# Sparse attention with two gated layers: measured durations for small TensorE tasks in the table that a planner orders the instructions by

## The chip, the cores and the metric

The kernel runs on one core of a Trainium2 chip. The metric is the time of one execution on the device in microseconds (us); where several runs were made, the median stands first and the lowest and highest behind it. Five instruction queues matter here: TensorE (PE, matrix products), VectorE (DVE), ScalarE (ACT), GpSimd (POOL, masks at the start only) and SyncE (SP), which issues nearly all DMA transfers.

## The reference

Four batches of 576 positions with 8 heads of 64 go through a sparse attention: heads 0 to 3 look at the last 32 positions, heads 4 to 7 at positions with the same remainder modulo 32. The 2304 x 512 result goes through a layer with a Mish-like gate (512 to 2048 to 512), and then through a layer that takes the maximum of three products (512 to 768, back to 512). The weights are 64-bit numbers, which the kernel reads as two 32-bit words; every operand of the large products is split into a high and a low part (three products for one).

```python
scores = scale * np.matmul(q, k.transpose(0, 1, 3, 2))
mask_local = (rel >= 0) & (rel < stride)
mask_strided = (rel >= 0) & (pos[None, :] % stride == pos[:, None] % stride)
attn = np.exp(scores - max);  attn = attn / sum;  x = np.matmul(attn, v)
h = x @ w_in;  x = (h * np.tanh(softplus(h))) @ w_out
h = np.maximum(np.maximum(x @ w1, x @ w2), x @ w3);  out = h @ w_out
```

## The kernel before

The kernel never lets a scheduler order its instructions. `build_plan` describes the whole computation as some thousands of tasks: each has an engine, a duration (`cost`, in ns), the buffers that it reads and writes, a rank, and a function that emits its instructions. `Plan.run` then plays the tasks through on paper, engine by engine, always taking the ready task of lowest rank, forwards and backwards in turn; the forward order that ends first on paper is emitted as it stands. So a duration in this table changes no instruction. It changes where in each engine's queue an instruction stands.

**The attention** is cut into 48 units: 4 batches, 4 pairs of heads, 3 units each, of 3 or 4 tiles. A unit keeps one PSUM bank (`a0`, `a1`, `a2`, `acc1`, `acc2` in turn) and goes through: scores on PE (L413, two products a tile, one for each head, side by side in a quarter of the array each: the tiled mode), mask and row maximum on DVE (L426, L432), exponentials on ACT (L438), normalisation on DVE (L445 to L451), a transpose on PE (L458), its copy on ACT (L463), the product with v on PE (L471, tiled mode again), and the split of the result on ACT and DVE (L489, L493). The trace shows each tiled product as two records. q and k are loaded and turned beforehand: for batch 0 through PE (L355, tiles `early`), for the others by a DVE transpose (L329, tiles `raw`).

**The first product of the gated layer** for the first four slices of w_in (L516 in 288 columns, banks `h0` and `acc3`, 384 instructions) only needs finished attention rows and converted weights, and the planner weaves it in between the small tasks. The last 72 of these come behind the attention. Then follow L543 and L516 (the gated layer) and L590 and L615 (the second layer) in long unbroken rows.

**Fills.** Where the plan sees PE waiting, it puts in products that compute nothing (L839, 128x256 into `acc0`, which nobody reads), as many as fit in the wait by its own clock; they are there to keep the engine active. No fill is put in once the first L543 has been planned.

**What the planner charges on PE**: the cost of the task, and `SWITCH` where a task that is not tiled follows a tiled one; until this change a transpose counted as small and was free of it. The way back into the tiled mode is charged nothing. For a wait between engines it uses the table `WAIT`.

Of the kernel before, what the change touches and what calls it, by code (L numbers as in the profile page):

```python
# [19 lines left out]
P = 128  # L20
# [14 lines left out]
RES = 3  # L35
ATT_BANKS = ("a0", "a1", "a2", "acc1", "acc2")
RAW_BANKS = ("h0", "acc3")
RING = dict(h=3, g=3, ev=4, wt=4, s=5, st=8, pt=3, raw=2, qT=2, v=2)
# [5 lines left out]
    pe=dict(pe=0, act=200, dve=210, pool=200, sp=200), act=dict(pe=260, act=140, dve=150, pool=200, sp=150),  # L44
# [3 lines left out]
for waits in WAIT.values():  # L48
    waits["qa"] = waits["sp"]
WAIT["qa"] = dict(WAIT["sp"])  # L50
SWITCH = 60
DMA_ISSUE, DMA_START, DMA_END = 475, 1125, 850
HAM, HAM_COLS = 10240 / 3, 3060
SMALL_MM = ("scores", "tp", "av", "qkt")
# [13 lines left out]
class Plan:  # L68
# [30 lines left out]
    def run(self, rank, backward):  # L99
        succ, pred = (self.pred, self.succ) if backward else (self.succ, self.pred)  # L100
        n = len(self.name)
        left = [len(p) for p in pred]
        ready, done = [0.0] * n, [0.0] * n
        free = dict.fromkeys(self.ENGINES, 0.0) if backward else dict(START)
        later = {e: [] for e in self.ENGINES}
        now_ready = {e: [] for e in self.ENGINES}
        for i in range(n):
            if not left[i]:
                heappush(later[self.eng[i]], (0.0, i))
        order, wire, busy, last, fill, count = [], 0.0, {}, None, True, 0  # L110
        table = "mish" if backward else "exp"
        while count < n:
            now, e = min(
                (free[e] if now_ready[e] else max(free[e], later[e][0][0]), j)
                for j, e in enumerate(self.ENGINES) if now_ready[e] or later[e]
            )
            e = self.ENGINES[e]
            while later[e] and later[e][0][0] <= now:
                i = heappop(later[e])[1]
                heappush(now_ready[e], (rank[i], i))  # L120
            if e == "pe" and last is not None:
                def worth(entry):
                    name = self.name[entry[1]]
                    same = name == last if last in SMALL_MM else name not in SMALL_MM
                    return entry[0] - STAY * same, entry[1]

                r, i = min(now_ready[e], key=worth)
                now_ready[e].remove((r, i))
                heapify(now_ready[e])
            elif e == "act":  # L130
                def late(entry):
                    t = TABLE.get(self.name[entry[1]], table)
                    return entry[0] + TABLE_STAY * (t != table), entry[1]

                r, i = min(now_ready[e], key=late)
                now_ready[e].remove((r, i))
                heapify(now_ready[e])
            else:
                i = heappop(now_ready[e])[1]
            cost = self.cost[i]  # L140
            if e == "act":
                t = TABLE.get(self.name[i], table)
                cost += TABLE_LOAD * (t != table)
                table = t
            if e in ("sp", "qa"):
                free[e] = now + DMA_ISSUE
                wire = max(wire, now + (0 if backward else DMA_START)) + cost
                done[i] = wire + (DMA_START if backward else 0) + DMA_END
            else:
                if e == "pe":  # L150
                    t, w = free[e], int(free[e] // HAM)
                    fill = fill and not backward and self.name[i] != "x2_mm"
                    while fill and t + (c := FILL / (2.4 if busy.get(w - 1, 0) >= HAM_COLS else 1.2)) + FILL_GAP <= now:
                        busy[w] = busy.get(w, 0) + FILL
                        order.append(-1)
                        t += c
                        w = int(t // HAM)
                    if last in TILED_MM and self.name[i] not in SMALL_MM:
                        cost += SWITCH
                    last = self.name[i]  # L160
                    if not backward:
                        w = int(now // HAM)
                        busy[w] = busy.get(w, 0) + self.cols[i]
                        cost *= 1 if busy.get(w - 1, 0) >= HAM_COLS else 2
                done[i] = free[e] = now + cost
            order.append(i)
            count += 1
            for j in succ[i]:
                wait = WAIT[self.eng[j]][e] if backward else WAIT[e][self.eng[j]]
                ready[j] = max(ready[j], done[i] + wait)  # L170
                left[j] -= 1
                if not left[j]:
                    heappush(later[self.eng[j]], (ready[j], j))
        return order, done, max(done)
# [15 lines left out]
def build_plan(k, B, H, S, D, DM, FF, FF2, wide):  # L190
# [120 lines left out]
    def attention():  # L311
        n = 0
        for i, (b, hp) in enumerate(pairs):
            local = hp < 2
            r = i % 2
            rv = i if i < RING["v"] + 2 else i % RING["v"]
            rk0 = unit_rank(n)
            lr = rk0 - 8 if b else -200 + i
            if not b:
                early_qk(i, b, hp, local, r, rk0, lr)  # L320
            for nm in ("q", "k") if b else ():
                for g in range(4):
                    add("qk_load", "sp", S * PACKET[128], (lambda g=g, nm=nm, b=b, hp=hp, r=r: k.load_qk(nm, g, b, hp, k.raw(nm, r))),
                        writes=[("raw", nm, r, g)], rank=lr)

                def tr(nm=nm, r=r, local=local):
                    t = k.qkT(nm, r)
                    tv = t.rearrange("p (j r) -> p j r", r=STRIDE) if local else t.rearrange("p (r j) -> p j r", j=NJ)
                    nc.vector.transpose(out=tv, in_=k.raw(nm, r))  # L329

                add("tr", "dve", 669, tr, reads=[("raw", nm, r, g) for g in range(4)], writes=[("qT", nm, r)], rank=rk0 - 0.5)
            vparts = k.v_parts(hp)
            for j in range(vparts):
                v_cost = PACKET[256] * (LK * (2 if j == 0 else NL - 1) if local else NJ * (NS - (j % RES == RES - 1)))
                add("v_load", "sp", v_cost, (lambda j=j, b=b, hp=hp, rv=rv: k.load_v(j, b, hp, k.v(rv))),
                    writes=[("v", rv, j_) for j_ in range(j, 2 * RES, vparts)], rank=lr + 0.5)
            for u, tiles in enumerate(unit_tiles[local]):
                unit(n, i, u, tiles, b, hp, local, r, rv)
                n += 1
            if i == H // 2 - 1:  # L340
                add("hrpool", "dve", 0, k.open_hrpool, writes=[("earlypool",)], rank=-1)
# [35 lines left out]
    def unit(n, i, u, tiles, b, hp, local, r, rv):  # L377
# [31 lines left out]
        for j, tl in enumerate(tiles):  # L409
            def scores(j=j, tl=tl):  # L410
                kw = LK if local else width(tl)
                for h in range(2):
                    nc.tensor.matmul(  # L413
                        ps()[LQ * h:LQ * h + width(tl), j * K:j * K + kw],
                        lhsT=cols("q", h, tl), rhs=cols("k", h, tl), start=True, stop=True,
                    )
            add("scores", "pe", 212 if local else 142, scores, reads=[("qT", "q", r), ("qT", "k", r)], writes=[bk], rank=rk, cols=4 * (K if local else width(tl)))

        def mask():
            if not local:  # L420
# [35 lines left out]
        for j in range(nt):  # L456
            def tp(j=j):
                nc.tensor.transpose(ps()[:K, j * P:j * P + rows], sv()[:, j, :], k.ident[:rows, :rows])  # L458
            add("tp", "pe", 108 if local else 100, tp, reads=[sk[j]], writes=[bk], rank=rk)
        w_ = (nt - 1) * P + rows  # L460

        def evac():
# [3 lines left out]
        for j, tl in enumerate(tiles):  # L466
            def av(j=j, tl=tl):
                w = width(tl)
                kw = LK if local else w
                for h in range(2):  # L470
                    nc.tensor.matmul(  # L471
                        ps()[D * h:D * (h + 1), j * M:j * M + w],
                        lhsT=k.v(rv)[:kw, h, tl, :], rhs=k.buf(pb)[:kw, j * P + LQ * h:j * P + LQ * h + w],
                        start=True, stop=True,
                    )
            add("av", "pe", 160, av, reads=[pk] + [("earlypool",)] * (rv >= RING["v"]) + [("v", rv, j_) for j_ in range(2 * RES)], writes=[bk], rank=rk, cols=8 * width(tl) * K / P)

        def io(part):
            xv = k.x[:, part, hp, b * S:(b + 1) * S]
# [411 lines left out]
```

## Time and profile before

| | |
|---|---|
| median of 3 runs | 801.79 us (799.7 to 802.49) |
| the profiled execution, own time | 803.02 us |
| its span, first to last instruction | 801.2 us |
| PE busy | 793.7 us (99%) |
| DVE busy, ACT busy | 361.0 us (45%), 321.1 us (40%) |
| granted TensorE clock, mean | 1.000 (the level of 2.4 GHz) |

The span has three stages. Up to about 143 us it is the attention with the woven-in products; from there to about 500 us the gated layer; from there to the end the second layer. A busy PE says little by itself, since pipelined products overlap in the records and fills count too: the starts of its instructions, and what it waited for, are the better guide.

### The profile page before, as it was taken

To read this page: it belongs to the slowest core of one execution; us is meant where nothing else is said; L and a number is where in the kernel's file an instruction comes from. 1 tells how busy PE (TensorE), PEld (TensorE's weight loads), DVE (VectorE), ACT (ScalarE), POOL (GpSimd) and SP (SyncE) were. 2 spreads that over 40 slices of the span, in tenths; PEclk is the share of its full clock that TensorE was granted. 3 is DMA by queue.
4 is the path that set the end of the run, shared out by engine and by line. 5 is a ranking of instruction groups with operands and counts; after the bars stand their busy time and mean duration, and the time that the engine had idled before them with its cause. 6 is when DMAs were issued, how large, how long until landed. Compare 5 with 4: busy or idle time off the path is not lost.

```text
span 801.2 us, 12605 instructions
## 1 busy us (share of the span) xinstructions
PE 793.7 (99%) x5017; PEld 670.4 (84%) x5017; DVE 361.0 (45%) x769; ACT 321.1 (40%) x839; POOL 4.4 (1%) x22
## 2 busy tenths in 40 slices
PE   9999999999999999999999999999999999999998
PEld 7878888988888888888888889888888888888897
DVE  6998886895941311311221169981222221122222
ACT  5988878996731322321322257631110111110111
POOL 2000000000000000000000000000000000000000
PEclk9999999999999999999999999999999999999999
DMA  9787750944900100100010069300100010010010
GB/s 212 156 158 125 134 105 22 351 149 163 334 2 1 53 0 1 54 0 1 1 53 0 1 224 325 109 1 0 53 1 0 13 41 1 0 53 1 0 53 27
DMA packets 119690, 59.66 MB, mean 74 GB/s; under 512 B 91984, under 2 KB 110416, under 8 KB 119632
## 3 DMA queue, kind: packets, MB, share of 16 engines
q1 hardware_dynamic: 118448, 58.57, 26.2%
q8 instruction: 39, 0.64, 0.3%
q10 hardware_dynamic: 1184, 0.30, 0.2%
q14 instruction: 19, 0.16, 0.1%
HBM read 49.41 MB, written 9.44 MB: 73 GB/s over the span
## 4 chain that ended last, share of the span: by engine, by line
PE 88%; DMA 4%; SPq 3%; DVE 3%; ACT 1%; issue 1%; DVEq 0%; ACTq 0%
PE bank_acc L543 23%; PE bank_a L590 21%; PE bank_a L516 12%; PE bank_acc L615 9%; PE bank_h L516 7%; PE bank_h L590 7%; PE bank_acc L516 3%; DMA wslot<-in_moe_w_dram 1%; DMA v<-in_v_dram 1%; PE bank_a L413 1%; PE bank_a L471 1%; SPq L809 1%; PE bank_a L458 1%; PE bank_acc L413 1%; PE bank_acc L471 1%; DMA wslot<-in_moe_w_out_dram 1%
## 5 line engine op out<-in xcount | busy, mean ns | idle before, releaser
L543 PE MATMUL bank_acc<-g,wslot 128*128 128x512 f32 (+1 forms) x960 | 205.1, 369 | 1.5 <-DVE g L538 0.7
L543 PEld LDWEIGHTS bank_acc<-g,wslot 128*128 128x128 f32 x960 | 168.3, 188 | 33.6 <-DVE g L538 2.0
L590 PE MATMUL bank_a<-x,wslot 128*128 128x512 f32 (+1 forms) x816 | 173.2, 367 | 0.0
L590 PEld LDWEIGHTS bank_a<-x,wslot 128*128 128x128 f32 x816 | 142.4, 189 | 25.5
L538 DVE TENSOR_TENSOR g<-h,g 128x512 fp32r<-128x512 f32 (+1 forms) x80 | 50.9, 636 | 192.1 <-ACT g L537 192.0
L516 PE MATMUL bank_a<-x,wslot 128*128 128x512 f32 (+1 forms) x540 | 116.2, 368 | 0.0
L516 PEld LDWEIGHTS bank_a<-x,wslot 128*128 128x128 f32 x540 | 94.6, 189 | 16.8
L599 DVE TENSOR_TENSOR h<-bank_a,h 128x512 f32<-128x512 f32 (+1 forms) x46 | 29.1, 633 | 137.3 <-PE bank_a L590 137.3
L615 PE MATMUL bank_acc<-wslot,g 128*128 128x512 f32 x324 | 78.3, 389 | 0.0
L516 PE MATMUL bank_h<-x,wslot 128*128 128x288 f32 (+2 forms) x372 | 74.2, 338 | 0.0
L615 PEld LDWEIGHTS bank_acc<-wslot,g 128*128 128x128 f32 x324 | 60.4, 188 | 12.3
L535 ACT ACTIVATE h<-bank_a 128x512 f32<-128x512 f32 (+1 forms) x45 | 25.0, 554 | 108.8 <-PE bank_a L516 108.8
L516 PEld LDWEIGHTS bank_h<-x,wslot 128*128 128x128 f32 x372 | 58.5, 188 | 7.1
L601 ACT ACTIVATE g<-h 128x512 fp32r<-128x512 f32 (+1 forms) x30 | 17.6, 588 | 114.9 <-DVE h L599 114.9
L590 PE MATMUL bank_h<-x,wslot 128*128 128x512 f32 (+1 forms) x264 | 58.3, 370 | 0.0
L438 ACT ACTIVATE s<-s,st 118x54 f32<-118x54 f32 (+1 forms) x160 | 55.2, 348 | 7.0 <-DVE st L432 6.7
L590 PEld LDWEIGHTS bank_h<-x,wslot 128*128 128x128 f32 x264 | 46.7, 188 | 8.6
L537 ACT CAST g<-h 128x512 fp32r<-128x512 f32 (+1 forms) x80 | 46.1, 577 | 4.4 <-PE bank_acc L543 2.6
L253 ACT ACTIVATE wt<-wslot 128x512 f32<-128x512 f32 x56 | 37.9, 678 | 21.6 <-DVE wslot L281 9.6
L277 ACT CAST wslot<-wt 128x512 fp32r<-128x512 f32 x56 | 34.3, 620 | 14.7 <-DVE wt L267 14.3
L596 ACT COPY h<-bank_a 128x512 f32<-128x512 f32 (+1 forms) x22 | 12.0, 547 | 69.0 <-PE bank_a L590 69.0
L281 DVE TENSOR_TENSOR wslot<-wt,wslot 128x512 fp32r<-128x512 f32 x56 | 38.2, 684 | 2.6 <-ACT wslot L277 2.5
(71 smaller groups left out, 680.2 us busy)
## 6 DMA issues: line engine op xcount, KB each, us to landing
wslot<-in_moe_w_out_dram SPq DMA_DIRECT2D x22, 512.0 KB
wslot<-in_moe_w_dram SPq DMA_DIRECT2D x18, 512.0 KB
wslot<-in_moe_w_in_dram SPq DMA_DIRECT2D x16, 512.0 KB
out_dram<-wt SPq DMA_DIRECT2D x18, 256.0 KB
x2p<-ev SPq DMA_DIRECT2D x16, 256.0 KB
ev<-x2p SPq DMA_DIRECT2D x16, 256.0 KB
rawq<-in_q_dram SPq DMA_DIRECT2D x48, 72.0 KB
rawk<-in_k_dram SPq DMA_DIRECT2D x48, 72.0 KB
```

What stands on the lines that cost most here:

```text
L253: nc.scalar.mul(k.wt(r2).bitcast(F32), k.words(slot)[1].bitcast(F32), 2.0 ** -111)
L277: nc.scalar.copy(out=k.open_slot(slot)[:, 0, :], in_=k.wt(r2).bitcast(F32))
L281: nc.vector.tensor_tensor(out=s[:, 1, :], in0=k.wt(r2).bitcast(F32), in1=s[:, 0, :], op=ALU.subtract)
L438: nc.scalar.activation(sv()[:, j, :], sv()[:, j, :], AF.Exp, bias=mx()[:, j:j + 1], accum_out=dn()[:, j:j + 1],)
L516: nc.tensor.matmul(k.bank(hb)[:, :n], lhsT=wap(("in", f), a, c), rhs=k.x[:, q, c, t0:t0 + n], start=(c == 0 and m == 0), stop=(c == KC - 1 ...
L535: add(name, "act", act(n, psum=not stored), lambda: nc.scalar.activation(Hh(), src(), AF.Mish, scale=W_SCALE), reads=sread, writes=[HK], r ...
L537: add("gh", "act", act(n), lambda: nc.scalar.copy(out=g()[:, 0, :n], in_=Hh()), reads=[HK], writes=[G0], rank=s)
L538: add("gl", "dve", dve(n), lambda: nc.vector.tensor_tensor(out=g()[:, 1, :n], in0=Hh(), in1=g()[:, 0, :n], op=ALU.subtract), reads=[HK, G0 ...
L543: nc.tensor.matmul(k.bank(f"acc{c}")[:, :n], lhsT=wap(("out", f), a, c), rhs=g()[:, q, :n], start=(first and m == 0), stop=(last and m == 2),)
L590: nc.tensor.matmul(k.bank(hb)[:, :n], lhsT=wap((w_, f), a, c), rhs=k.x[:, q, c, t0:t0 + n], start=(c == 0 and m == 0), stop=(c == KC - 1 a ...
L599: add("m2", "dve", dve(n), (lambda hb=hb: nc.vector.tensor_tensor(out=m_(), in0=k.bank(hb)[:, :n], in1=m_(), op=ALU.max)), reads=[("bank", ...
L615: nc.tensor.matmul(k.bank(ab)[:], lhsT=k.g(rg)[:, a, c * P:(c + 1) * P], rhs=t[:, q, :], start=(f == 0 and m == 0), stop=(f == F2C - 1 and ...
```

## The change

Four kinds of tasks get other durations, and two lines of the mode change are altered. Scores fall from 212 or 142 ns a tile to 96 or 56, products with v from 160 to 64; transposes on PE rise from 108 or 100 to 124 or 106, the DVE transpose from 669 to 760 or 1200. `SWITCH` rises from 60 to 90 and is now charged ahead of a transpose too. No instruction of the computation is added or removed.

```diff
-SWITCH = 60
+SWITCH = 90
-                    if last in TILED_MM and self.name[i] not in SMALL_MM:
+                    if last in TILED_MM and self.name[i] not in TILED_MM:
                         cost += SWITCH
-                add("tr", "dve", 669, tr, reads=[("raw", nm, r, g) for g in range(4)], writes=[("qT", nm, r)], rank=rk0 - 0.5)
+                add("tr", "dve", 760 if local else 1200, tr, reads=[("raw", nm, r, g) for g in range(4)], writes=[("qT", nm, r)], rank=rk0 - 0.5)
-            add("scores", "pe", 212 if local else 142, scores, ...
+            add("scores", "pe", 96 if local else 56, scores, ...
-            add("tp", "pe", 108 if local else 100, tp, ...
+            add("tp", "pe", 124 if local else 106, tp, ...
-            add("av", "pe", 160, av, ...
+            add("av", "pe", 64, av, ...
```

What the planner makes of it: up to the last 72 products L516 behind the attention the order is another one on every engine; from there on all queues are the same, word for word. Fills (L839) rise from 61 to 168; 107 more, all of them in this first part.

PE, batch 0, around the transposes of the fourth pair's q (`earlyq_96`), before:

```order
L839 MATMUL bank_acc_105<-x 128x256 x7
L471 MATMUL bank_a_101<-pt_124,v_134 64x64 x6
L458 MATMUL bank_a_102<-ident,s_110 54x118 x4
L839 MATMUL bank_acc_105<-x 128x256 x7
L355 MATMUL bank_h_104<-ident,earlyq_96 128x96 x3
L355 MATMUL bank_acc_108<-ident,earlyk_97 128x96 x3
L458 MATMUL bank_a_103<-ident,s_111 54x118 x4
L839 MATMUL bank_acc_105<-x 128x256 x3
```

The same place, after:

```order
L839 MATMUL bank_acc_105<-x 128x256 x7
L471 MATMUL bank_a_101<-pt_124,v_134 64x64 x6
L839 MATMUL bank_acc_105<-x 128x256 x15
L355 MATMUL bank_h_104<-ident,earlyq_96 128x96 x3
L839 MATMUL bank_acc_105<-x 128x256 x13
L458 MATMUL bank_a_102<-ident,s_110 54x118 x4
L355 MATMUL bank_h_104<-ident,earlyq_96 128x96 x3
L839 MATMUL bank_acc_105<-x 128x256 x3
```

Between the same products with v and the same end of the turning there are 10 fills before (7 and 3) and 31 after.

PE, some 20 rows on, at the first scores of batch 1 (`bank_a_103`), before:

```order
L471 MATMUL bank_acc_106<-pt_124,v_135 64x54 x4
L471 MATMUL bank_acc_106<-pt_124,v_135 64x36 x2
L516 MATMUL bank_h_104<-x,wslot 128x288 x3
L413 MATMUL bank_a_103<-qTk_131,qTq_129 64x96 x6
L516 MATMUL bank_h_104<-x,wslot 128x288 x3
L516 MATMUL bank_acc_108<-x,wslot 128x288 x6
```

The same place, after:

```order
L471 MATMUL bank_acc_106<-pt_124,v_135 64x54 x4
L471 MATMUL bank_acc_106<-pt_124,v_135 64x36 x2
L839 MATMUL bank_acc_105<-x 128x256 x19
L413 MATMUL bank_a_103<-qTk_131,qTq_129 64x96 x6
L839 MATMUL bank_acc_105<-x 128x256 x8
L458 MATMUL bank_acc_107<-ident,s_113 54x118 x4
```

Where products of the gated layer stood, 27 fills stand now; some of those products moved ahead, the others behind.

SP, the loads ahead of the fourth pair's q (`wslot` are slices of w_in, 512 KB each; `early` q and k, `v` values), before:

```order
L790 DMA wslot_233<-in_moe_w_in_dram 128x4x256
L820 DMA v1_134<-in_v_dram 96x2x64
L826 DMA v1_134<-in_v_dram 96x8x64 x2
L790 DMA wslot_255<-in_moe_w_in_dram 128x4x256
L834 DMA v2_135<-in_v_dram 18x11x64 x2
L834 DMA v2_135<-in_v_dram 18x10x64
L809 DMA earlyq3_96<-in_q_dram 96x6x64 x2
```

The same stretch, after:

```order
L790 DMA wslot_249<-in_moe_w_in_dram 128x4x256
L826 DMA v1_134<-in_v_dram 96x8x64 x2
L790 DMA wslot_278<-in_moe_w_in_dram 128x4x256
L790 DMA wslot_282<-in_moe_w_in_dram 128x4x256
L834 DMA v2_135<-in_v_dram 18x11x64 x2
L790 DMA wslot_311<-in_moe_w_in_dram 128x4x256
L834 DMA v2_135<-in_v_dram 18x10x64
L809 DMA earlyq3_96<-in_q_dram 96x6x64 x2
```

Four slices of w_in now stand ahead of that load, where there were two.

## Rows read from the trace of the kernel before

**Rows 1.** The page: busy time by engine; granted clock in 40 slices.

```profile
PE 793.7 (99%) x5017; PEld 670.4 (84%) x5017; DVE 361.0 (45%) x769; ACT 321.1 (40%) x839; POOL 4.4 (1%) x22
...
PEclk9999999999999999999999999999999999999999
```

**Rows 2.** Stretches: length, busy PE, PEld, DVE, ACT, POOL, clock, DMA, GB/s.

```profile
0.00:12.70 12.70, 10.96 (x73) 9.65 (x74) 5.58 (x13) 3.66 (x10) 4.39 (x22) 1.00 1.00 194
12.70:60.00 47.30, 46.95 (x653) 38.51 (x651) 45.22 (x139) 41.80 (x172) 0.00 (x0) 1.00 0.84 170
60.00:143.50 83.50, 83.32 (x1142) 71.04 (x1139) 65.09 (x196) 67.61 (x283) 0.00 (x0) 1.00 0.53 101
143.50:153.10 9.60, 9.60 (x74) 9.60 (x74) 8.01 (x15) 9.43 (x21) 0.00 (x0) 1.00 1.05 381
...
465.00:501.00 36.00, 34.86 (x276) 33.52 (x276) 31.13 (x62) 24.37 (x51) 0.00 (x0) 1.00 0.93 308
...
760.00:801.20 41.20, 37.43 (x267) 35.00 (x265) 9.73 (x21) 6.42 (x15) 0.00 (x0) 1.00 0.11 39
```

**Rows 3.** All waits of PE for other engines: us in total, times, longest.

```profile
PE bank_acc L839 <- DVE x L855: 1.2, 1, 1.2
PE bank_acc L543 <- DVE g L538: 0.7, 2, 0.5
PE bank_h L355 <- DMA earlyq<-in_q_dram: 0.6, 1, 0.6
PE bank_acc L543 <- ACT g L537: 0.5, 2, 0.3
```

**Rows 4.** Timeline of PE behind the attention: start, duration, instructions.

```profile
142.49 1.12 PE L839 MATMUL bank_acc<-x 128*128 128x256 f32 x8
143.45 1.75 PE L516 MATMUL bank_h<-x,wslot 128*128 128x288 f32 x12
...
153.01 1.31 PE L543 MATMUL bank_acc<-g,wslot 128*128 128x512 f32 x5
```

**Rows 5.** Timeline of PE from 60 us.

```profile
60.01 0.66 PE L516 MATMUL bank_acc<-x,wslot 128*128 128x288 f32 x3
60.60 0.57 PE L471 MATMUL bank_a<-pt,v 96*64 96x64 f32 x12
61.10 1.07 PE L516 MATMUL bank_h<-x,wslot 128*128 128x288 f32 x6
62.10 0.61 PE L413 MATMUL bank_a<-qTk,qTq 64*54 64x54 f32 x16
```

**Rows 6.** Timeline of PE from 12 us.

```profile
12.74 1.19 PE L839 MATMUL bank_acc<-x 128*128 128x256 f32 x8
13.78 0.41 PE L355 MATMUL bank_acc<-ident,earlyk 96*128 96x96 f32 x3
...
14.66 0.49 PE L458 MATMUL bank_a<-ident,s 128*96 128x128 f32 x3
15.07 0.88 PE L413 MATMUL bank_acc<-qTk,qTq 64*64 64x96 f32 x16
```

**Rows 7.** The chain of waits in order of time: start, length, what.

```profile
12.31 1.71 SPq L790
...
26.46 0.50 SPq L790
...
59.36 3.40 DMA v<-in_v_dram
...
80.19 0.33 PE bank_a L458 x3
...
134.09 0.94 PE bank_acc L471 x28
```

**Rows 8.** PE by line and form: busy, mean ns, idle before.

```profile
L839 PE MATMUL bank_acc<-x 128*128 128x256 f32 x61 | 12.0, 337 | 1.2 <-DVE x L855 1.2
```

**Rows 9.** DVE by line and form.

```profile
L329 DVE STREAM_TRANSPOSE qTk<-rawk 128x576 f32<-128x576 f32 x12 | 12.1, 1007 | 0.6 <-DMA v<-in_v_dram 0.6
```

More of the change, by code (lines that the diff above doesn't have):

```diff
@@ L416, in scores @@
                     )
-            add("scores", "pe", 212 if local else 142, scores, reads=[("qT", "q", r), ("qT", "k", r)], writes=[bk], rank=rk, cols=4 * (K if local else width(tl)))
+            add("scores", "pe", 96 if local else 56, scores, reads=[("qT", "q", r), ("qT", "k", r)], writes=[bk], rank=rk, cols=4 * (K if local else width(tl)))
         def mask():
@@ L458, in tp @@
                 nc.tensor.transpose(ps()[:K, j * P:j * P + rows], sv()[:, j, :], k.ident[:rows, :rows])
-            add("tp", "pe", 108 if local else 100, tp, reads=[sk[j]], writes=[bk], rank=rk)
+            add("tp", "pe", 124 if local else 106, tp, reads=[sk[j]], writes=[bk], rank=rk)
         w_ = (nt - 1) * P + rows
@@ L475, in av @@
                     )
-            add("av", "pe", 160, av, reads=[pk] + [("earlypool",)] * (rv >= RING["v"]) + [("v", rv, j_) for j_ in range(2 * RES)], writes=[bk], rank=rk, cols=8 * width(tl) * K / P)
+            add("av", "pe", 64, av, reads=[pk] + [("earlypool",)] * (rv >= RING["v"]) + [("v", rv, j_) for j_ in range(2 * RES)], writes=[bk], rank=rk, cols=8 * width(tl) * K / P)
         def io(part):
```

## The prediction

> **What bounds the kernel now.** I read the page first, then the stretches, the waits of PE, and its timeline at a few places. The page gives PE 99% busy at the full granted clock in all 40 slices [rows 1], against 45% and 40% on DVE and ACT. Busy time of PE proves little, so the waits come next: in the whole execution PE waited 3.0 us for other engines (1.2 + 0.7 + 0.6 + 0.5), and 1.2 of these are the very start [rows 3]. In the stretches PE idles 0.35 us between 12.7 and 60 us and 0.18 us up to 143.5; later it loses some 1.1 us at 465 to 501 us and 3.8 us at the very end [rows 2]. The starts agree. In the timeline each row begins where the steps of the one before end: the 72 products L516 behind the attention take 153.01 - 143.45 = 9.56 us, 0.133 each [rows 4], and three or six of them between tiled products take 0.59 and 1.00 us, which is 3 x 0.133 and 6 x 0.133 plus 0.2 for the change of mode [rows 5]. So in the attention stage PE is not merely busy but out of slack: the end of that stage (143.45 us, where the last 72 products L516 begin) is the sum of what stands in its queue, plus the start.
>
> DVE and ACT are close behind in one part: 45.2 and 41.8 us of 47.3 between 12.7 and 60 us, and 65 and 68 of 83.5 behind it [rows 2]. And up to 59.36 us the chain of work runs through SP and transfers of v, not through PE [rows 7]. Both are near limits, but neither makes PE wait today.
>
> **What the change does to PE's queue.** No product is added or taken away; only the order of the first part changes, and from the 72 products on all queues are the same. So the rest, 801.2 - 143.45 = 657.7 us of the span, is carried over as it is, and the question is how long the first part gets. Its PE work is the same 312 products L516, the same scores, transposes and products with v; what differs is fills and changes of mode.
>
> Fills: 168 where there were 61. Eight of them take 143.45 - 142.49 = 0.96 us from start to start [rows 4], 0.12 each. The mean of one record is 337 ns and the group's busy time 12.0 us for 61 [rows 8]; these are no prices, since neighbours overlap in the records and the first fills wait. 107 x 0.12 = **+12.8 us**. The low bound is the pace of L516 for fewer columns, 0.133 x 256 / 288 = 0.118 us, so 12.6 us; the high bound are the eight near the start, 13.78 - 12.74 = 1.04 us [rows 6], 0.13 each, so 13.9 us.
>
> Changes of mode: the queue leaves the tiled mode and comes back 77 times before and 71 times after. The price of such a trip depends on what is in it. Through products L516: coming back costs 0.59 - 3 x 0.133 = 0.19 us; leaving shows as six pairs L471 in 0.50 us [rows 5], where 14 pairs in one piece take 0.94 [rows 7], so eight pairs more cost 0.44, a pair 0.055, and leaving 0.50 - 6 x 0.055 = 0.17. Together 0.36. Through transposes alone: three of them take 15.07 - 14.66 = 0.41 us ahead of scores [rows 6] and 0.33 ahead of a product [rows 7], so coming back is 0.08 to 0.1, with the leaving 0.27. Trips that end from a product or a fill rise from 41 to 54, those that end from a transpose fall from 36 to 17: 13 x 0.36 - 19 x 0.27 = **-0.4 us**. The bounds are -2.2 us (six trips fewer at 0.36 each, if all cost alike) and 13 x 0.36 - 19 x 0.17 = +1.4 us (if the way back from a transpose is free).
>
> In sum PE's queue gets **12.4 us longer**. A rule would put this lower: the Trainium skill, TensorEngine Tiling (Array Packing), Key Properties, says that a change of the tiling mode drains the engine, which by itself counts every trip alike; with six trips fewer at 0.36 us the sum would be 12.8 - 2.2 = 10.6 us. The rows agree that a change costs time, yet a trip through transposes is cheaper than one through products.
>
> **Why the planner does it.** Between 12.7 and 143.45 us PE really spends 130.75 us, of which 312 x 0.133 = 41.5 go to L516 and 44 x 0.12 = 5.3 to fills, so 84 us to the small tasks with their mode changes. The old table charged 27.8 us for scores (72 tiles and 88), 25.6 for products with v (160), 16.6 for transposes, 2.9 for turning q and k and 2.6 for 43 switches, 75 in all. The new one charges 11.8, 10.2, 18.3, 2.9, and 71 x 0.09 = 6.4, 50 in all. The durations are true for a product in a row of its kind, but the way back into the tiled mode has no price, and it is what the old numbers were padded with. The plan now sees a PE with some 25 us more room than before, finds waits, and fills them. On the chip PE is later than the plan thinks, so the things that the fills wait for are there by then.
>
> **Other terms.** The dearer DVE transpose is near the truth (12.1 us for 12, 1007 ns each over both kinds [rows 9], against 669) and costs nothing by itself. Two slices of w_in more stand ahead of the fourth pair's q on SP. One is 512 KB: at 381 GB/s (143.5 to 153.1 us) [rows 2] 1.4 us, at the 194 GB/s of the start 2.7 us; the issue itself takes 0.50 to 1.71 us [rows 7]. So that q lands 2.8 to 5.4 us later. What hides it: 70 fills instead of 31 stand ahead of its first use, 39 x 0.12 = 4.7 us, and some small tasks that used to stand behind it are ahead of it now; PE did not wait there before. So 0 us; if the cover were gone, up to 5.4 us. DVE and ACT have the same work in a stage that is 12.4 us longer, so they lose slack nowhere on the mean.
>
> Against the profiled execution: 803.02 + 12.4 = 815.4 us. That execution lies 1.2 us over the median; against the median of the runs it is 801.79 + 12.4 = **814.2 us**.
>
> **The rivals.**
> A, fills in time and new waits on top. The loads and the conversions of w_in moved ahead in the stretch where DVE is 96% busy [rows 2] and the chain runs through loads [rows 7]. If PE comes to q, or to the rows that DVE normalises, before they are ready, it waits up to 5.4 us more: 814.2 + 5.4 = 819.6 us. Against it speaks that PE itself is later at every step.
> B, the fills lie in the shade. If PE in truth waits up to 59.36 us for what the chain shows there, fills only take the place of waits. 81 of the 107 lie ahead of the same products with v that start at 60.60 us; with these for nothing 26 x 0.12 = 3.1 us are left: 804.9 us. Against it: recorded starts follow each other at constant steps there, and the list of waits has 0.6 us for a load in all [rows 3].
> C, the new order is better, and **faster**. Fills would have to cost next to nothing, slipping into the draining at a change of mode as tiled pairs run side by side; then six trips fewer (-2.2 us) and the waits of PE behind the start (-1.8 us) [rows 3] would show: 797.8 us. It decides at 2.2 / 107 = 0.02 us a fill; the timeline has 0.12 [rows 4].
> D, nothing moves: the planner's table is not what bounds, and the order differs in ways that cancel. It needs the same shade as B and the gains of C: 801.8 us.
> Nor can more fills win a higher clock: it is 1.00 in all stretches with 61 of them [rows 2].
>
> **How the numbers follow.** The forecast (fills paid in full, no new wait) 0.78; A 0.12; B 0.04; D 0.03; C 0.03. The forecast's own bounds: 12.6 - 2.2 = 10.4 us and 13.9 + 1.4 = 15.3 us, so 812.2 to 817.1 us, and 811.5 to 818 with what a median of few runs scatters (the three lie 2.8 us apart). With the larger part of A the range is 811.5 to 819. A measurement of this kernel tells some 0.3% (2.4 us) from no change. Faster by more 0.03 (C), within 0.03 (D), slower 0.94.
>
> **What would show it.** In the profile after, the last 72 products L516 should begin at about 156 us instead of 143.45, L543 9.6 us behind them, and the stretches behind should have the old lengths. The L839 group should have 168 instructions; its rows in the timeline should keep 0.12 us a fill; PE's waits should stay at about 3 us. DVE and ACT should have the same busy time and more waits for PE. The prediction is wrong if the first part grows by much less than the fills (B) or if waits for early q, for L451 or for L463 appear on PE (A).

## The result, and the profile after

| | before | after |
|---|---|---|
| median | 801.75 us (799.7 to 802.67, six executions) | 811.19 us (808.47 to 812.39, six executions) |
| the profiled execution, own time | 803.02 us | 808.47 us |
| its span | 801.2 us | 806.7 us |
| last 72 products L516 begin | 143.45 us | 149.97 us |

The changed kernel is slower: ratio 1.0112, interval 1.0098 to 1.0126, which is 9.4 us. The forecast was 12.4 us more (814.2 us, range 811.5 to 819.0): right in sign and in the main cause, 3.0 us too much, and the time lies 0.3 us below the range. The two profiled executions are 5.5 us apart only: that of before (803.02 us) lies above all six in the table, and that of after is the shortest of its six; the section on the experiments shows a good part of why.

The page of after: busy time by engine, granted clock in 40 slices, and the chain that ended last by engine; the first two rows of before are [rows 1].

```profile
PE 799.8 (99%) x5124; PEld 680.6 (84%) x5124; DVE 358.8 (44%) x769; ACT 322.1 (40%) x839; POOL 4.4 (1%) x22
...
PEclk9999999999999999999999999999999999999999
...
PE 95%; DMA 2%; DVE 1%; ACT 1%; SPq 0%; issue 0%; ACTq 0%
```

107 more instructions on PE, the same numbers of instructions on DVE and ACT and nearly their busy time: nothing else was added. The chain, which still ran through loads for part of the early stage before [rows 7], is PE for 95% now. On the page of before that row reads:

```profile
PE 88%; DMA 4%; SPq 3%; DVE 3%; ACT 1%; issue 1%; DVEq 0%; ACTq 0%
```

All waits of PE in after (us in total, times, longest), for [rows 3]:

```profile
PE bank_acc L839 <- DVE x L855: 1.2, 1, 1.2
PE bank_h L355 <- DMA earlyq<-in_q_dram: 0.6, 1, 0.6
PE bank_acc L543 <- DVE g L538: 0.5, 2, 0.4
PE bank_acc L355 <- DVE qTk L370: 0.3, 1, 0.3
PE bank_acc L355 <- DMA earlyk<-in_k_dram: 0.2, 1, 0.2
PE bank_acc L543 <- ACT g L537: 0.2, 1, 0.2
```

3.0 us in sum, as before. The load of q that the prediction worried about is in the list with the same 0.6 us.

Stretches of after (length, then busy PE, PEld, DVE, ACT, POOL with their instructions, granted clock, DMA share, GB/s), for [rows 2]:

```profile
12.70:60.00 47.30, 47.30 (x653) 41.81 (x650) 40.57 (x126) 38.21 (x158) 0.00 (x0) 1.00 0.82 166
60.00:150.00 90.00, 90.00 (x1225) 78.33 (x1224) 65.95 (x204) 71.08 (x290) 0.00 (x0) 1.00 0.51 96
150.00:159.60 9.60, 9.60 (x75) 9.60 (x74) 8.18 (x15) 9.42 (x21) 0.00 (x0) 1.00 1.05 383
```

From 12.7 us on PE has no idle time at all in the attention (0.35 and 0.18 us before). DVE fell from 45.22 to 40.57 us of 47.3: with more fills on PE the small tasks go by more slowly, so DVE has less to do per us.

Timeline of PE in after behind the attention (start, duration, instructions), for [rows 4]:

```profile
148.55 1.58 PE L839 MATMUL bank_acc<-x 128*128 128x256 f32 x12
149.97 1.74 PE L516 MATMUL bank_h<-x,wslot 128*128 128x288 f32 x12
...
159.54 0.85 PE L543 MATMUL bank_acc<-g,wslot 128*128 128x512 f32 x3
```

Twelve fills from 148.55 to 149.97, 0.118 each; the 72 products in 9.57 us (9.56 before); and behind their start 806.7 - 149.97 = 656.7 us of the span (657.7 before). So the difference arises ahead of the 72 (6.5 us), as forecast, but they were expected at about 156 us. The 1.0 us less behind them is scatter: a second execution of before, further down, has 656.2 us there with the same queues.

### The profile page after: what moved, and what is told of

The parts are those of the page before. It is cut to its first block, busy times and chain, and to the rows that moved or that the text cites. A ratio compares the mean times of both kernels' runs of the same rounds, so it can differ in the third digit from the quotient of the medians.

```text
span 806.7 us, 12825 instructions
## 1 busy us (share of the span) xinstructions
PE 799.8 (99%) x5124; PEld 680.6 (84%) x5124; DVE 358.8 (44%) x769; ACT 322.1 (40%) x839; POOL 4.4 (1%) x22
## 4 chain that ended last, share of the span: by engine, by line
PE 95%; DMA 2%; DVE 1%; ACT 1%; SPq 0%; issue 0%; ACTq 0%
PE bank_acc L543 23%; PE bank_a L590 21%; PE bank_a L516 13%; PE bank_acc L615 9%; PE bank_h L516 8%; PE bank_h L590 7%; PE bank_acc L516 4%; PE bank_acc L839 3%; PE bank_a L413 2%; PE bank_a L471 2%; PE bank_a L458 2%; PE bank_acc L413 1%; PE bank_acc L471 1%; DMA wslot<-in_moe_w_in_dram 1%; PE bank_acc L458 1%; DMA wslot<-in_moe_w_dram 1%
## 5 line engine op out<-in xcount | busy, mean ns | idle before, releaser
L516 PE MATMUL bank_a<-x,wslot 128*128 128x512 f32 (+1 forms) x540 | 116.2, 368 | 0.0
L516 PEld LDWEIGHTS bank_a<-x,wslot 128*128 128x128 f32 x540 | 94.6, 189 | 16.8
L516 PE MATMUL bank_h<-x,wslot 128*128 128x288 f32 (+2 forms) x372 | 74.5, 338 | 0.0
L516 PEld LDWEIGHTS bank_h<-x,wslot 128*128 128x128 f32 x372 | 58.6, 188 | 6.9
L253 ACT ACTIVATE wt<-wslot 128x512 f32<-128x512 f32 x56 | 37.9, 678 | 19.4 <-DVE wslot L281 9.4
```

Source lines behind the costliest of these rows:

```text
L253: nc.scalar.mul(k.wt(r2).bitcast(F32), k.words(slot)[1].bitcast(F32), 2.0 ** -111)
L516: nc.tensor.matmul(k.bank(hb)[:, :n], lhsT=wap(("in", f), a, c), rhs=k.x[:, q, c, t0:t0 + n], start=(c == 0 and m == 0), stop=(c == KC - 1 ...
```

## The experiments

Theory 1, the prediction's: fills and changes of mode are paid, and nothing else. Theory 2: the fills keep the granted clock up, so taking them out loses what it gains. Theory 3: the new order makes PE wait, and its fills stand in waits that would otherwise show.

**One part of the change alone, the durations of scores and products with v.** 166 fills.

```diff
-            add("scores", "pe", 212 if local else 142, scores, ...
+            add("scores", "pe", 96 if local else 56, scores, ...
-            add("av", "pe", 160, av, ...
+            add("av", "pe", 64, av, ...
```

> One part alone: scores and products with v get their new durations, everything else as before. The order has 166 fills (after: 168) and 79 trips out of the tiled mode (after: 71). Theory 1, the fills that a cheaper PE brings are the change's cost: 105 x 0.119 = 12.5 us of fills, 2 trips more at 0.25, less 1 to 4 us of small waits that vanish: 809 to 814 us. Rival, the cost comes from the mode rule and the transposes: 802 us.

Measured: 812.5 us, ratio 1.0141 (1.0124 to 1.0159), clock 1.000. These two lines alone cost 11.3 us over the 801.15 us of before in that session, more than the whole change.

**The rest of the change alone** (transposes dearer on PE and DVE, `SWITCH` 90, also charged ahead of a transpose). 62 fills, one more than before.

```diff
-SWITCH = 60
+SWITCH = 90
-                    if last in TILED_MM and self.name[i] not in SMALL_MM:
+                    if last in TILED_MM and self.name[i] not in TILED_MM:
-                add("tr", "dve", 669, tr, ...
+                add("tr", "dve", 760 if local else 1200, tr, ...
-            add("tp", "pe", 108 if local else 100, tp, ...
+            add("tp", "pe", 124 if local else 106, tp, ...
```

> The other parts alone: the mode rule at 90 ns ahead of transposes too, the new durations of transposes on PE and DVE; scores and products with v keep their old durations. 62 fills and 74 trips (before: 61 and 77). Theory 1: 0.1 us of fills, three trips fewer at 0.25, so 800 to 802.5 us. Rival, the cost of the change comes from these parts: 811 us.

Measured: 804.58 us, ratio 1.0045 (1.0030 to 1.0059). A miss: nearly as many fills and three trips (out of the tiled mode and back) fewer, and yet 3.4 us more than before. So the two parts do not add up: 11.3 and 3.4 us alone, 9.4 us together, each with an order of its own. Two rows of this kernel go with the miss, a stretch (columns as above) and its longest wait behind the start:

```profile
20.00:40.00 20.00, 18.79 (x247) 15.75 (x246) 16.12 (x51) 16.73 (x71) 0.00 (x0) 0.83 0.79 159
```

```profile
PE bank_a L471 <- DMA v<-in_v_dram: 1.1, 1, 1.1
```

PE waits 1.1 us for v; that wait ends at 30.96 us, and from about 31.5 to 38.3 us the granted clock is 0.50 (1.2 GHz instead of 2.4), which makes the mean of this stretch 0.83. All five executions have a mean clock of 0.993 to 0.995.

**The order of before, with only the first 17 of its 61 fills**

```diff
+        fills.append(1)
+        if len(fills) > 17:
+            return
```

> The order of before; of its 61 fills only the first 17 are emitted, the other 44 (which compute nothing that is read) are left out. Theory 1, fills are paid in full on PE: 44 x 0.119 = 5.2 us less than 801.75, so 796.5 us. Theory 2, the fills stand where PE would wait anyway: 801.7 us, and PE's list of waits grows by some 5 us. Theory 3, without them the granted clock falls below 1.00 in a stretch before 143 us, and the time comes out above 801.7 us.

Measured: 805.24 us, ratio 1.0046 (1.0030 to 1.0062), where theory 1 had 796.5 us: 44 fills less, and slower. Its stretch:

```profile
20.00:40.00 20.00, 15.43 (x209) 12.06 (x205) 15.56 (x52) 15.16 (x69) 0.00 (x0) 0.83 0.86 158
```

PE is idle for 4.6 us there, and behind a wait of 1.7 us for ACT (L471 for the copy L463, ending at 32.70 us) the clock is at half from about 33 to 39.7 us. Fills are no pure loss: where they stood there are now waits, and a lower clock.

**The order of after, with only the first 17 of its 168 fills** (the same edit).

> The order of after; of its 168 fills only the first 17 are emitted, 151 are left out. Theory 1, paid in full: 151 x 0.119 = 18.0 us less than 811.19, so 793.2 us, some 3 us below the other order without its fills (fewer changes of mode, fewer small waits). Theory 2, the fills stand where PE would wait: 811 us and long waits of PE for transfers, DVE and ACT. In between, what is lacking from 18.0 us is the share of the fills that stands for waits of the new order. Theory 3 as in the other kernel: a granted clock below 1.00 before 150 us.

Measured: 811.33 us, ratio 1.0124 (1.0103 to 1.0145). 151 fills, some 18 us of PE time at 0.119 each, were taken out and the time did not move. Stretches, and the longest waits of PE:

```profile
20.00:40.00 20.00, 15.04 (x209) 12.52 (x207) 15.79 (x48) 15.03 (x57) 0.00 (x0) 0.74 0.79 147
40.00:60.00 20.00, 18.05 (x179) 14.25 (x181) 14.61 (x42) 13.80 (x61) 0.00 (x0) 0.66 0.70 136
```

```profile
PE bank_a L458 <- DVE s L451: 2.8, 3, 2.3
PE bank_a L413 <- DVE st L445: 1.6, 1, 1.6
PE bank_acc L543 <- ACT g L537: 1.5, 1, 1.5
```

The waits that the plan saw in the new order are real: in the attention 2.8 us for the rows that DVE normalises (L451), 1.6 us for another step of DVE (L445). During the first and behind the second the clock falls: it is at half from 27.7 to 37.9 and from 41.3 to 55.0 us, 24 us in all. Theory 1 falls as a statement about this order; theories 2 and 3 hold.

**The order of before, with 107 fills more** (each fill behind the first 17 emitted three or four times, at its place), 168 as in after.

```diff
+        n = len(fills) - 18
+        for _ in range(1 if n < 0 else 3 + ((n + 1) * 19 // 44 > n * 19 // 44)):
+            fill_one()
```

> The order of before, with 107 more fills that compute nothing: each fill behind the first 17 is emitted three or four times, so 168 as after. No task is moved. Theory 1, a fill costs its 0.119 us in full: 801.2 + 12.7 = 813.9 us. Theory 2, the small waits of PE that its list doesn't show (2.8 us by the sum of steps) are filled by them: 811 us. Rival, most of them stand in the shade of loads and of DVE, as the chain of waits up to 59 us suggests: 802 to 806 us.

Measured: 812.91 us, ratio 1.0148 (1.0135 to 1.0162), 11.75 us over before, so 0.110 per fill. This is the prediction's first term by itself, with the order held still: 92% of it is paid. The interval (10.8 to 13.0 us) would allow all of it. The traces narrow that down: a row behind the rise of the clock, and the start of the 72 products, in this kernel and then in a second execution of before (its own paragraph follows below):

```profile
22.13 0.47 PE L355 MATMUL bank_acc<-ident,earlyk 96*128 96x96 f32 x3
...
154.29 1.74 PE L516 MATMUL bank_h<-x,wslot 128*128 128x288 f32 x12
```

```profile
18.74 0.47 PE L355 MATMUL bank_acc<-ident,earlyk 96*128 96x96 f32 x3
...
142.14 1.74 PE L516 MATMUL bank_h<-x,wslot 128*128 128x288 f32 x12
```

From the same row to the 72 it is 132.16 us here, with 114 fills, and 123.40 there, with 33; in the first execution of before, where the row starts at 19.85, it is 123.60. So 81 fills cost 8.6 to 8.8 us, 0.107 each, against 0.119 from start to start in a row of fills: about a tenth is not paid. All waits of PE:

```profile
PE bank_acc L847 <- DVE x L863: 1.2, 1, 1.2
PE bank_h L355 <- DMA earlyq<-in_q_dram: 0.7, 1, 0.7
PE bank_acc L543 <- DVE g L538: 0.5, 2, 0.3
PE bank_acc L543 <- ACT g L537: 0.2, 1, 0.2
```

Behind the start there is 1.4 us of waits, against 1.8 us in before [rows 3]: the fills displaced next to nothing that the list shows, and what they did displace stands in no list.

**The changed kernel once more**, beside it.

> The kernel after once more, unchanged. In the profiled executions the granted clock rose from 1.2 to 2.4 GHz at 12.6 us (before) and at 5.4 us (after), though both kernels run the same instructions on PE up to 8 us. Theory: that moment is a matter of the execution, not of the change; so it lies anywhere in the first 13 us here, and the runs scatter by some 3 us, around 811 us. Rival: the new order lets the clock rise early; then it rises at 5 to 6 us again and the runs lie near 808.5 us.

Measured: 810.77 us, ratio 1.0117 (1.0097 to 1.0136), 9.61 us over before. At 168 fills each, the new order is 812.91 - 810.77 = 2.1 us better than the old one; each of the eleven executions of after (807.88 to 812.39) is shorter than each of the four of that kernel (812.68 to 813.41).

**The order of after, its fills thinned evenly to 61**

```diff
+        n = len(fills) - 18
+        if n >= 0 and (n + 1) * 44 // 151 == n * 44 // 151:
+            return
```

> The order of after with 61 fills, as many as before: behind the first 17 only 44 of 151 are emitted, evenly spread. Theory 1, the fills are paid in full and are all that the change costs: 811.2 - 12.7 = 798.5 us at a granted clock of 1.00. Theory 2, the new order by itself makes PE wait (for the loads, conversions and turned q and k that moved), and the fills only cover it: 805 to 811 us, with waits of some 6 us or more in PE's list, and a granted clock below 1.00 in the stretch where they were.

Measured: 805.13 us, ratio 1.0055 (1.0038 to 1.0071). With as many fills as before, the new order is 4.0 us slower than the old one; and its 107 further fills cost 810.77 - 805.13 = 5.6 us, 0.053 each, half of what they cost in the old order. For the other half there are waits: the list of waits of PE has 8.7 us in all here, 5.7 more than in after. Two of them, and the stretch:

```profile
PE bank_h L355 <- DMA earlyq<-in_q_dram: 2.5, 2, 1.8
...
PE bank_a L413 <- DVE st L445: 0.8, 1, 0.8
```

```profile
20.00:40.00 20.00, 16.70 (x229) 14.51 (x227) 16.40 (x49) 15.71 (x62) 0.00 (x0) 0.83 0.80 147
```

Here is the price of the moved loads: the fourth pair's q, which both kernels take without a wait, costs 1.8 us once fewer fills stand ahead of it, and the half clock sets in during that wait (28.4 to 35.3 us) in this execution. Not in all: two others, with a mean clock of 1.000, took 805.29 and 806.55 us, so the 4 us come without that dip too.

**The new durations, with the changes of mode priced as well** (leaving the tiled mode 205 ns, 120 ahead of a transpose; 90 ns for the way back). 108 fills, 78 trips.

```diff
-                        cost += SWITCH
+                        cost += 120 if self.name[i] in SMALL_MM else 205
+                    elif last not in TILED_MM and self.name[i] in TILED_MM:
+                        cost += 90
```

> The new table with the changes of mode priced as the steps of PE show them: leaving the tiled mode 0.205 us to a product or a fill and 0.12 to a transpose, coming back 0.09. The order has 108 fills and 78 trips. Theory: the fills come from what the new table leaves out; 47 x 0.119 = 5.6 us over before, so 805 to 807 us at a clock of 1.00. Rival, fills don't matter and the order alone does: 800 to 802 or 811 us.

Measured: 805.2 us, ratio 1.0053 (1.0038 to 1.0068), clock 1.00 in the profiled execution: inside the expected 805 to 807 us, at its low end. It is 4.0 us over before, 0.086 for each of the 47 fills and not 0.119; and since kernels with 61 and 62 fills in other orders took 805.1 and 804.6 us, the time alone does not show that fills are what is paid here. With the missing prices in the plan, 5.6 of the 9.6 us that the change costs are gone; but a more truthful plan is not yet a faster kernel.

**Three tables with fewer fills than before**, as candidates for a version that beats both kernels: only the dearer transposes on PE (52 fills, 74 trips); only the price and the rule of the change of mode (48 fills, 80 trips); and the change with its sign turned round, scores and products with v made dearer (40 fills, 76 trips).

```diff
+            add("tp", "pe", 124 if local else 106, tp, ...
```

> The planner gets only the dearer transposes on PE (124 and 106 ns for 108 and 100); all else is as before. PE's queue then has 52 fills, 9 fewer than before, and 74 trips out of the tiled mode, 3 fewer. Theory 1 (fills and changes of mode are paid, nothing else): 9 x 0.11 + 3 x 0.25 = 1.7 us less, 799.4 us, clock 1.00. Theory 2 (below some number of fills the clock falls, as with 17 and with 62 fills in other orders): one dip of the granted clock to half of 5 us or more between 20 and 60 us, and 803 to 805 us.

```diff
+SWITCH = 90
+                    if last in TILED_MM and self.name[i] not in TILED_MM:
```

> Only the price and the rule of the mode change are altered (90 instead of 60, charged ahead of transposes too). 48 fills, 80 trips. Theory 1: 13 x 0.11 - 3 x 0.25 = 0.7 us less than before, 800.4 us, clock 1.00. Theory 2: half clock somewhere between 20 and 60 us and 802.5 to 805 us.

```diff
+            add("scores", "pe", 260 if local else 180, scores, ...
+            add("av", "pe", 200, av, ...
+                add("tr", "dve", 693 if local else 1091, tr, ...
```

> The edit to the planner with the opposite sign: scores and products with v are made dearer instead of cheaper (260 and 180, 200 ns), transposes and the mode rule as in the change, the DVE transpose at the steps that its starts show (693 and 1091 ns). 40 fills, 76 trips. Theory 1: 21 x 0.11 + 1 x 0.25 = 2.6 us less than before, 798.5 us, clock 1.00. Theory 2: a half-clock stretch between 20 and 60 us and 803 to 807 us.

Measured: 804.86 us (ratio 1.0033, 1.0013 to 1.0052), 805.39 us (1.0043, 1.0025 to 1.0061) and 809.91 us (1.0093, 1.0077 to 1.0110), against 801.61 us. All slower; the second lies 0.4 us and the last 2.9 us above what theory 2 had. The last has 6.5 us of waits behind the start in its list (1.8 in before) and half clock from 41.4 to 51.7 us; what each of these costs is not shown. The first shows what goes with a half-clock stretch. Its stretch, and the timeline of PE in it:

```profile
40.00:60.00 20.00, 18.04 (x191) 14.33 (x189) 15.64 (x43) 12.30 (x48) 0.00 (x0) 0.83 0.82 157
```

```profile
41.61 0.55 PE L413 MATMUL bank_a<-qTk,qTq 64*64 64x96 f32 x8
44.01 1.31 PE L516 MATMUL bank_h<-x,wslot 128*128 128x288 f32 x3 [1.85 <-ACT x L489]
45.24 0.91 PE L471 MATMUL bank_a<-pt,v 96*64 96x64 f32 x12
...
51.39 0.67 PE L516 MATMUL bank_h<-x,wslot 128*128 128x288 f32 x3
51.98 0.38 PE L413 MATMUL bank_a<-qTk,qTq 64*64 64x96 f32 x4
```

PE waits 1.85 us for the rows that ACT writes. From 44.3 us on the clock is 0.50, and three products L516 with a change of mode take 1.23 us (44.01 to 45.24) where they take 0.59 once the clock is back, at 51.2 us (51.39 to 51.98). This kernel was executed twelve times, and the clock tells the executions apart: five with a mean of 1.000 took 801.41 to 803.20 us, seven with 0.993 to 0.996 took 804.49 to 807.61. Between the medians of the two groups, 802.9 and 805.9, lie 3.0 us: an estimate of what one such stretch costs, with whatever else differed between them (only one of the twelve left a trace). And with the clock at 1.000, 9 fills and 3 trips fewer have still won nothing (802.9 against 801.6).

**The kernel before once more, for its trace**

> The kernel before once more, for its trace. If the moment at which the clock first rises is a matter of the execution and not of the order, it need not be at 12.6 us again; between 4 and 13 us, and the start of the last 72 products L516 moves with it, from 140 to 144 us. If it belongs to the order, it is at 12.6 us again and the 72 begin at 143.4 us. In both cases PE waits some 3 us in all behind the start.

Measured: 800.11 us. The 72 products begin at 142.14 us, where they began at 143.45 in the execution above, although all queues are the same. Stretch of the start, in this execution; in the first one the same stretch reads 1.00 [rows 2]:

```profile
0.00:12.70 12.70, 10.33 (x83) 9.37 (x84) 6.38 (x16) 4.66 (x14) 4.40 (x22) 0.87 1.00 189
```

The timeline of PE in that first execution of before, and in after, gives both away:

```profile
8.86 3.15 PE L413 MATMUL bank_a<-qTk,qTq 64*64 64x96 f32 x36
11.93 0.74 PE L355 MATMUL bank_h<-ident,earlyq 96*128 96x96 f32 x3
```

```profile
7.94 1.21 PE L413 MATMUL bank_a<-qTk,qTq 64*64 64x96 f32 x24
9.08 0.47 PE L355 MATMUL bank_acc<-ident,earlyk 96*128 96x96 f32 x3
```

36 scores in 3.07 us, 0.085 each, before; 24 in 1.14 us, 0.048 each, after. Before ran them at 1.2 GHz, after at 2.4. The view says 1.00 for both, since it takes the clock as full until the first change that is recorded, and in before that first change is the rise, at 12.6 us. When the clock first rises is a matter of the execution: at 5.4 us in after, at 4.8 in its second profile, at 10.7 in the kernel with 107 more fills; the second execution of before even rises at 4.2, falls at 7.6 and rises again at 11.0 us. A mean clock has the same blind spot: it leaves out what lies ahead of the first recorded change, and the 0.998 of this execution is the fall at 7.6 us alone, not a dip later on. With 10 fills and three transposes more behind it, some 1.5 us of work, after stands at 11.92 us where before stands at 12.74: 0.82 + 1.5, so an estimated 2.3 us of luck between the two profiles.

## Why the prediction was wrong by a little, point by point

**The cause** was right in the main. The fills come from the two durations of scores and products with v, they stand ahead of the 72 products, and the time is lost there. Two terms of the sum failed: the changes of mode, -0.4 us where the order gave -2.1, are 1.7 us of the miss; the fills, +12.8 us where 11.75 were measured, are 1.05. How much falls to the order and how much to the fills hangs on what is altered first: at 168 fills the new order gains 2.1 us and the fills cost 11.75 in the old one; at 61 fills the new order loses 4.0 us and the fills cost 5.6 in it. The sum is 9.6 us either way. So the prediction's picture, one price for a fill and no new waits, holds for the old order nearly and for the new one only as long as its fills stand there.

**The fills, +12.8 us**: mis-sized, because PE was not quite out of slack. The size of one was right (0.118 to 0.12 in the timeline). With the order held still, 107 of them cost 11.75 us (lined-up traces: 0.107 each). What takes the missing 1.05 us would be waits that are too short for the list, which shows none below 0.2 us; that rests on an estimate. From the steps between all starts of the traces: when products, fills and changes of mode have each their one price, 3.7 us are left over in the first part of before, 2.7 in the kernel with 107 more fills in that order, and 0.9 in after. With other prices for the same steps 4.5, 3.6 and 2.4 us are left, so the order of the three is safer than the sizes. The list of waits, on which the prediction built "0.35 and 0.18 us idle", does not see these, since neighbouring instructions overlap in the records. The low bound of this term (12.6 us) was a bound on the length of a fill, and left out that part of it may be hidden. The term of the changes of mode came out near its low bound of -2.2 us, and so the time fell out of the range, by 0.3 us.

**The changes of mode, -0.4 us**: the larger failure. After against the old order with equally many fills is -2.1 us. By the same estimate a trip's price hangs on what follows the leaving: 0.12 us to leave, 0.106 on top if a product or a fill comes first, 0.033 if a transpose does, and 0.09 for the way back. So a trip that starts with a product costs 0.32 us and one that starts with a transpose 0.24; the prediction's 0.36 and 0.27 were not far off, but it sorted the trips by what stands at their end. At its own prices the sorting by the start would have given 0.36 - 7 x 0.27 = -1.5 us. Sorted by their start, product or fill go from 43 to 44 and transposes from 34 to 27, so 6 x 0.21 - 0.106 + 7 x 0.033 = 1.4 us are saved (the estimate over every single step gives 1.1). What is left of the 2.1 us would be short waits that the new order with its fills has less of (2.7 against 0.9 us in the estimate above); no run shows this part by itself. That 11.75 - 2.1 = 9.65 us is the 9.6 measured is no proof of the two terms, since both were taken from the runs; the 9.4 us of the first six executions are the independent number. The Trainium skill, TensorEngine Tiling (Array Packing), Key Properties, says that a change of the tiling mode drains the engine, and gives no price. Read as one price for every trip it gave -2.2 us and would have come nearer in size; the steps agree that a change costs time, but do not show every trip alike.

**The start of the 72 products** was forecast at 156 us against the profiled execution and came at 149.97, 5.9 us early: 1.05 for the fills, 1.7 for the order, and 2.3 for the clock at the start, which is a matter of the execution; 0.8 us stay open. The clock "1.00 in all stretches" [rows 2] was misread for the first of them, and so was the mean of 1.000 in the table of before: its first 12.6 us, ahead of the recorded rise, ran at half clock by the pace of the scores.

**The loads, 0 us** was right, and so was the cover that the prediction named: with 61 instead of 168 fills the fourth pair's q makes PE wait 1.8 us.

**Why the planner does it** was right in its first half: cheap small tasks alone bring 166 fills. That the missing way back is what the old numbers were padded with explains a part: with all changes of mode priced there are 108 fills, not 61. Its last sentence, that what the fills wait for is there by then, holds for half of the fill time at most: with 107 of them out again 5.6 of 12.7 us came back, with 151 out nothing.

**The rivals.** A (new waits) did not come in the changed kernel, because its own fills cover them; without them they come. B (fills in the shade) is wrong for the old order, at 0.110 a fill, and half right for the new one, at 0.053. C had the sign of the order right, by 2.1 us, and the price of a fill wrong. D fell with the result. "Nor can more fills win a higher clock" was right for this change: means of 0.998 to 1.000 in after's executions. What it missed is the other direction. Of before's twenty executions beside the last four kernels two had a mean clock of 0.994, and took 804.46 and 804.78 us (a third took 804.55 at 1.000). None of the eleven of after fell below 0.998; that is too few to say that its fills protect it.

No kernel of this study beat the one before.

## What to carry to other kernels

Before fills are counted as cost (or taken out as waste), hold the order still and multiply them, then thin them: the same 107 cost 11.75 us in one order and 5.6 us in the other. A list of waits that sums to almost nothing may still leave a few us in gaps that are too short for it (an estimate here); a low bound has to allow for them. A change of mode is counted by what follows it, not by what ends the trip. And a table that a planner orders by is a whole: every kernel with a truer number here or there was slower, with new fills or with new waits, and a wait of PE of 1 to 2 us may go with another 3 us through the clock.

## What the runs showed of the hardware

- Each of the seven profiles with half clock between 12.7 and 143 us has a wait of PE of 1.1 to 2.3 us that ends shortly before the fall or lies across it (in the one shown the wait ends at 44.01 us and the fall comes at 44.3), and the half clock lasts 3 to 14 us. The profiles of before, after and the other kernels with 108 and more fills have no wait over 0.6 us in that stretch, and no fall. The Trainium skill, TensorE: Matmul & The Clock Gate, HAM oscillation — how this bites in real kernels, tells of waits for transfers that throw the clock back, so that the next piece of work starts slow. The traces agree in kind, not in size: the page's example has waits of some 3 to 5 us, here 1.1 to 2.3 us went with the fall, and six of the eight waits were for VectorE or ScalarE.
- It is no matter of such a wait alone. Four profiles fall at 7.6 to 8.1 us, where the longest wait of PE since the rise had been 0.7 to 0.9 us and had ended over 2 us earlier. And the same queues with the same data kept 1.000 in five executions and fell in seven; whether their waits differed is not known.
- At half clock a score takes 0.085 us instead of 0.048, and three products L516 1.23 instead of 0.59 us.
- The first rise of the clock came between 4.2 and 12.6 us, at 4.2 and at 12.6 with the very same queues, and moves the end by up to some 2 us (an estimate); single profiles of two kernels should be lined up behind it.
